# Attention weights applied to the tokens before Wv, Wv as the stationary operand, one pool of PSUM banks and a new order of stages

## The chip, the cores and the metric

The kernel runs on one core of one Trainium2 chip. The metric is the device time of one execution in microseconds. The engines are named as the profile names them: PE (TensorE, matmuls), PEld (its weight loads), DVE (VectorE), ACT (ScalarE), POOL (GpSimd) and SP (SyncE, which issues the weight DMAs).

## The reference

Four blocks run one after the other on x of shape 2048 x 640: memory attention A, local attention B, A again, B again. Each adds its result to x after a layer norm.

```python
# A: segments of 32 tokens, 8 memory tokens ahead of each; 32 heads of 192
for s in range(n_seg):                                # 64 segments
    h = concat([mem, xs], axis=1)                     # 40 x 640
    q, k, v = h @ Wq, h @ Wk, h @ Wv                  # per head 40 x 192
    scores = q @ k.T * scale                          # masked
    p = softmax(scores)                               # per head 40 x 40
    o = (p @ v) @ Wo                                  # sum over heads
    mem = o[:, :8, :]                                 # carried to the next segment
    outs.append(o[:, 8:, :])
# B: 32 heads of 20; each token attends to 8 positions, 2 apart
q, k, v = split(x @ wqkv)
o = softmax(sum(q * k[window])) * v[window] @ wo
```

The memory makes segment s + 1 of a block wait for segment s of the same block.

## The kernel before

One step handles one segment of both A blocks at once: segment s of the first and segment s - 2 of the second (`LAG`), as two "lanes" `l` of 40 rows, 80 columns in all. The state `ST` holds the tokens of both lanes transposed, 5 chunks of 128 features. There are 67 steps; the last one does B alone. The weights of A, 64 halves of 128 x 1920 bf16 (480 KB), don't fit: 31 stay in SBUF (`RESIDENT`), the other 33 are read again in each step through a ring of 5 buffers (`half`, L227 to L241, DMAs on SP's queue). In step 0 all come from the inputs, and the streamed ones are written to DRAM as they will be read (`Wr`).

The stages of a step, each named in `PLAN`:

- `q` (qk, 16 of them, two heads each): queries and keys; weights stationary, the 80 columns of `ST` moving; 30 matmuls; ACT copies the bank to a `QK` tile (L315).
- `s` (scores, 4, each for four q): 32 matmuls on parts of the array (L325, L331), then a softmax chain on DVE and ACT (L335 to L343) that ends in `Pm`.
- `t` (p_transpose, 4): four PE transposes, `Pm` to `PT`, copied out by DVE and then ACT (L352, L353).
- `v` (16): `ST` stationary, a half of Wv moving, 5 matmuls of 384 columns (L361); ACT or DVE copies out by turns (L365, L367).
- `pv` (4): v stationary in pieces of 64 columns, `PT` moving, 24 half-tile matmuls (L378) for two `ot` tiles, 96 in a step; ACT copies out (L381).
- `o` (16): a half of Wo stationary, `ot` moving, summed up in one PSUM tile `acc` over the whole step (L395).
- B, for the segments that the step before has finished: `ln1` (b_stats), `qkv`, `logits`, `e` (b_expand, 5), `wo`, `ln2` (beta_x), `store`; and `alpha` and `input` for new tokens.

PE runs in the order of `PLAN` as written (`manual_schedule(engines={PE})`). The other engines' orders are made at build time by the framework's scheduler from its own estimate of when each instruction is ready; at run time each engine goes through its queue in order. `COLUMNS` is a table of costs that only chooses which halves stay resident, so that the streamed ones are spread evenly over a step. PSUM has eight banks: pool psA has three (q, v and acc), psS three (s and pv), psB two (everything else). At the end of a step `finish_step` (L398) casts the memory rows of `acc` into the next `ST` (L405).

Of the kernel before, what the change touches and what calls it, by code (L numbers as in the profile page):

```python
# [10 lines left out]
BF16 = mybir.dt.bfloat16  # L11
F32 = mybir.dt.float32
# [3 lines left out]
PSUM = bass.MemoryType.PSUM  # L16
# [3 lines left out]
P = 128  # L20
D = 640
NCH = 5
# [3 lines left out]
NM = 8  # L26
SEG = 32
LT = NM + SEG
SLOT = 64
NP_ = 16  # L30
UW = 384
# [18 lines left out]

def stages():

    plan = [("q", 0), ("q", 1), ("alpha", 0), ("q", 2), ("q", 3), ("ln1", 0)]
    plan += [("q", 4), ("s", 0), ("v", 0), ("q", 5), ("v", 1), ("qkv", 0), ("q", 6), ("t", 0), ("v", 2), ("q", 7), ("v", 3)]
    for g in (2, 3):
        i, j = 4 * g, 2 * (g - 2)
        extra = [[], [], [("logits", 0)], [("input", 0)], []] if g == 2 else [[("e", c)] for c in range(5)]
        plan += [("q", i), ("s", g - 1), ("pv", g - 2)] + extra[0] + [("v", i - 4)] + extra[1] + [("q", i + 1)] + extra[2]
        plan += [("o", 2 * j), ("o", 2 * j + 1)] + extra[3] + [("v", i - 3), ("q", i + 2), ("t", g - 1), ("v", i - 2)] + extra[4]
        plan += [("o", 2 * j + 2), ("o", 2 * j + 3), ("q", i + 3), ("v", i - 1)]  # L60
    plan += [("s", 3), ("pv", 2), ("v", 12), ("v", 13), ("wo", 0), ("o", 8), ("o", 9), ("v", 14), ("v", 15), ("t", 3)]
    plan += [("o", 10), ("ln2", 0), ("pv", 3), ("o", 11), ("store", 0)]
    return plan + [("o", k) for k in range(12, 16)]
# [5 lines left out]
COLUMNS = {"q": 1200, "v": 1920, "o": 1200, "s": 2000, "pv": 1000, "t": 700, "ln1": 900, "ln2": 900, "qkv": 5000, "logits": 1000, "e": 500, "wo": 1700}  # L69


def resident_halves():

    order, t = [], 0
    for what, i in PLAN:
        for h in ([2 * i, 2 * i + 1] if what == "q" else [{"v": 32, "o": 48}[what] + i] if what in "vo" else [None]):
# [40 lines left out]
class Kernel:  # L117
    def __init__(self, ctx, tc, A_x, A_mem0, A_Wq, A_Wk, A_Wv, A_Wo, B_wqkv, B_wo, out):
        self.tc, self.nc = tc, tc.nc
        self.x = A_x[0, :, :]  # L120
        self.out = out[0, :, :]
        self.S = A_x.shape[1]
        self.n_seg = self.S // SEG
        self.Wq, self.Wk, self.Wv = (w.rearrange("d h e -> d (h e)") for w in (A_Wq, A_Wk, A_Wv))
        self.Wo = A_Wo.rearrange("h e d -> (h e) d")
        self.B_wqkv, self.B_wo, self.mem0 = B_wqkv, B_wo, A_mem0[0, :, :]
        pool = lambda name, bufs, **k: ctx.enter_context(tc.tile_pool(name=name, bufs=bufs, **k))
        self.cp = pool("consts", 1)
# [12 lines left out]
    def constants(self):  # L141
# [56 lines left out]
        self.PT = [cp.tile([P, 4, 2, 2, LT], BF16, name=f"PT{i}") for i in range(2)]  # L198
        for t in self.PT:
            nc.gpsimd.memset(t[:], 0.0)  # L200
# [5 lines left out]
        mt = self.psB.tile([P, NCH, NM], BF16, name="mt", tag="B")  # L206
# [46 lines left out]
    def input_tile(self, t):  # L253
# [12 lines left out]
        for k, src in enumerate((xn, x_sb)):  # L266
            tp = self.psB.tile([P, NCH, P], BF16, name="tp", tag="B")
# [12 lines left out]
    def ln_stats(self, src, n):  # L280
# [5 lines left out]
        ps = self.psB.tile([P, 2, n], F32, name="ln_ps", tag="B")  # L286
# [18 lines left out]
    def qk(self, i):  # L305
        nc = self.nc
        st = self.ST[self.step % 2]
        ps = self.psA.tile([P, 6, 2, LT], F32, name="qk_ps", tag="A")
# [8 lines left out]
    def scores(self, g):  # L317
        nc = self.nc
        ps = self.psS.tile([P, 4, 2, LT], F32, name="s_ps", tag="S")
# [14 lines left out]
        sb = self.w2.tile([P, 8, LT], F32, name="sb")  # L334
# [10 lines left out]

    def p_transpose(self, g):
        nc = self.nc
        ps = self.psB.tile([P, 4, 2, SLOT], BF16, name="pt_ps", tag="B")
        for j in range(4):
            nc.tensor.transpose(out=ps[:, j, :, :].rearrange("p h q -> p (h q)"),  # L350
                                in_=self.Pm[g % 2][:, j, :, :].rearrange("p l t -> p (l t)"), identity=self.ident[:, :])
        nc.vector.tensor_copy(out=self.PT[g % 2][0:64, :, :, 0, :], in_=ps[0:64, :, :, 0:LT])  # L352
        nc.scalar.copy(out=self.PT[g % 2][64:128, :, :, 1, :], in_=ps[64:128, :, :, 0:LT])  # L353

    def v(self, i):
        nc = self.nc
        w = self.half(32 + i)[:, :].rearrange("p (c n) -> p c n", c=NCH)
        st = self.ST[self.step % 2]
        ps = self.psA.tile([P, UW], F32, name="v_ps", tag="A")
        for c in range(NCH):  # L360
            nc.tensor.matmul(ps[:, :], lhsT=st[:, c, :, :].rearrange("p l t -> p (l t)"), rhs=w[:, c, :],  # L361
                             start=(c == 0), stop=(c == NCH - 1))
        vt = self.vp.tile([P, UW], BF16, name="vt")
        if i % 2 == 0:
            nc.scalar.copy(out=vt[:, :], in_=ps[:, :])  # L365
        else:
            nc.vector.tensor_copy(out=vt[:, :], in_=ps[:, :])  # L367
        self.vts[i] = vt

    def pv(self, g):  # L370
        nc = self.nc
        for k in (2 * g, 2 * g + 1):
            ps = self.psS.tile([P, 2, 3, 2, LT], F32, name="o_ps", tag="S")
            for jj in range(2):
                i = 2 * k + jj
                vt = self.vts.pop(i)
                for (n, slot, h, col) in ((0, 0, 0, 0), (0, 1, 0, 64), (1, 0, 0, 128), (1, 1, 1, 192), (2, 0, 1, 256), (2, 1, 1, 320)):
                    nc.tensor.matmul(ps[64 * slot:64 * (slot + 1), jj, n, :, :], lhsT=vt[:, col:col + 64], rhs=self.PT[g % 2][:, i % 4, h, :, :],  # L378
                                     start=True, stop=True, tile_position=(0, 64 * slot))
            ot = self.w3.tile([P, 6, 2, LT], BF16, name="ot")  # L380
            nc.scalar.copy(out=ot[:, :, :, :], in_=ps[:, :, :, :, :].rearrange("p j n l t -> p (j n) l t"))  # L381
            self.ots[k] = ot

    def o(self, jh):

        nc = self.nc
        j = jh // 2
        if jh == 0:
            self.acc = self.psA.tile([P, NCH, 2, LT], F32, name="acc", tag="A")
        ot = self.ots[j]  # L390
        for m in range(3 * (jh % 2), 3 * (jh % 2) + 3):
            if m % 3 == 0:
                w = self.half(48 + jh)[:, :].rearrange("p (m d) -> p m d", m=3)
# [30 lines left out]
    def b_qkv(self):  # L424
        nc = self.nc
        qT = self.w1.tile([P, NCH, 2, SEG], BF16, name="qT", tag="q")
        kh = self.w2.tile([P, NCH, 2, BPAD + SEG], BF16, name="kh")
        vh = self.w2.tile([P, NCH, 2, BPAD + SEG], BF16, name="vh")
        for new, old in ((kh, self.kh), (vh, self.vh)):
            if old is None:  # L430
                nc.gpsimd.memset(new[:, :, :, 0:BPAD], 0.0)
            else:
                nc.gpsimd.tensor_copy(out=new[:, :, :, 0:BPAD], in_=old[:, :, :, SEG:SEG + BPAD])
        for kind, dst in enumerate((qT[:, :, :, :], kh[:, :, :, BPAD:], vh[:, :, :, BPAD:])):
            ps = self.psB.tile([P, NCH, 2, SEG], F32, name="qkv_ps", tag="B")
# [5 lines left out]
        self.qT, self.kh, self.vh = qT, kh, vh  # L441
# [6 lines left out]
    def b_logits(self):  # L448
        nc = self.nc
        hf = SEG // 2  # L450
        ps = self.psB.tile([P, BW, hf], F32, name="lg_ps", tag="B")
# [25 lines left out]
    def b_expand(self, c):  # L477
        nc = self.nc
        ps = self.psB.tile([P, 2, BW, SEG], F32, name="bc_ps", tag="B")
# [7 lines left out]
    def b_wo(self):  # L487
        nc, s = self.nc, self.step
        ps = self.psB.tile([P, NCH, 2, SEG], F32, name="y_ps", tag="B")
# [22 lines left out]
    def store(self):  # L512
# [4 lines left out]
        ps = self.psB.tile([P, NCH, P], BF16, name="yt_ps", tag="B")  # L517
# [7 lines left out]
    def run(self):  # L525
        nc, tc = self.nc, self.tc
        self.resident, self.xt, self.vts, self.ots = {}, {}, {}, {}
        self.Wr = {h: self.dram.tile([P, HALF], BF16, name=f"Wr{h}") for h in range(N_HALVES) if h not in RESIDENT}
        self.kh = self.vh = None
        self.x2 = self.x2_next = None  # L530
        self.step = 0
        with tc.manual_schedule(engines={PE}):
# [5 lines left out]
            attend = {"q": self.qk, "s": self.scores, "t": self.p_transpose, "v": self.v, "pv": self.pv, "o": self.o}  # L538
            local = {"ln1": self.b_stats, "qkv": self.b_qkv, "logits": self.b_logits, "wo": self.b_wo, "ln2": self.beta_x, "store": self.store}
            for s in range(n_steps + 1):  # L540
# [10 lines left out]
                for what, i in PLAN:  # L551
                    if what in attend and a:
                        attend[what](i)
                    elif what in local and b:
# [64 lines left out]
```

## Time and profile before

| | |
|---|---|
| median of 3 runs | 3730.98 us (3726.68 to 3731.62) |
| span of the profiled execution | 3732.1 us; the page lists no time around it |
| PE busy | 3430.9 us (92%), 78045 matmuls |
| PEld busy | 2929.7 us (79%) |
| DVE busy | 2077.9 us (56%) |
| ACT busy | 1493.5 us (40%) |
| POOL busy | 365.5 us (10%) |
| granted PE clock | 0.984 on average, 1.00 from 200 to 3700 us |
| DMA | 1121.56 MB, 301 GB/s |
| casts of L405 that end the first and the last step with A | 144.89 and 3701.97 us |

Durations of one instruction are in its row of the page or of the groups by line and shape: 203 ns for a matmul of 80 columns, for example. Matmuls are pipelined, so a row's duration is not what one more of them costs; that is the distance from start to start, which the timeline gives. In the timeline, instructions of one kind that follow each other are merged into one row with their count, and the idle time before it stands in brackets with the engine that ended it.

### The profile page before, as it was taken

To read this page: it belongs to the slowest core of one execution; us is meant where nothing else is said; L and a number is where in the kernel's file an instruction comes from. 1 tells how busy PE (TensorE), PEld (TensorE's weight loads), DVE (VectorE), ACT (ScalarE), POOL (GpSimd) and SP (SyncE) were. 2 spreads that over 40 slices of the span, in tenths; PEclk is the share of its full clock that TensorE was granted. 3 is DMA by queue.
4 is the path that set the end of the run, shared out by engine and by line. 5 is a ranking of instruction groups with operands and counts; after the bars stand their busy time and mean duration, and the time that the engine had idled before them with its cause. 6 is when DMAs were issued, how large, how long until landed. Compare 5 with 4: busy or idle time off the path is not lost.

```text
span 3732.1 us, 170184 instructions
## 1 busy us (share of the span) xinstructions
PE 3430.9 (92%) x78045; PEld 2929.7 (79%) x78045; DVE 2077.9 (56%) x4858; ACT 1493.5 (40%) x3213; POOL 365.5 (10%) x467
## 2 busy tenths in 40 slices
PE   5799999999999999999999999999999999999997
PEld 3588788788788878778887887887888788788886
DVE  1355555655555555655556565555555555555555
ACT  1243444444444344444434444444443444444443
POOL 2110010011011001011100100100110010011000
PEclk7899999999999999999999999999999999999998
DMA  9988888888888889889888888888888888888885
GB/s 351 343 297 296 295 302 304 297 305 293 304 301 302 304 296 306 297 299 307 300 307 301 303 301 291 307 291 303 305 301 302 303 307 297 306 296 300 304 304 193
DMA packets 356064, 1121.56 MB, mean 301 GB/s; under 512 B 36424, under 2 KB 78032, under 8 KB 355344
## 3 DMA queue, kind: packets, MB, share of 16 engines
q1 hardware_dynamic: 350400, 1091.82, 86.2%
q0 software_dynamic: 2640, 16.22, 1.1%
q8 instruction: 610, 9.99, 1.1%
q10 hardware_dynamic: 2304, 2.62, 0.2%
q14 instruction: 110, 0.90, 0.1%
HBM read 1091.68 MB, written 18.84 MB: 298 GB/s over the span
## 4 chain that ended last, share of the span: by engine, by line
PE 66%; DVE 21%; DMA 7%; ACT 2%; issue 2%; SPq 1%; POOLq 0%; DVEq 0%; POOL 0%; ACTq 0%
PE qk_ps L313 23%; PE v_ps L361 18%; PE acc L395 11%; DVE oT L485 5%; DVE prod L483 4%; PE qkv_ps L438 4%; PE s_ps L331 3%; PE s_ps L325 2%; DVE vt L367 2%; PE o_ps L378 2%; DMA x_sb<-in_A_x_dram 2%; DMA wt<-Wr 2%; PE y_ps L492 1%; DVE sb L335 1%; DVE mx L337 1%
## 5 line engine op out<-in xcount | busy, mean ns | idle before, releaser
L315 ACT CAST QK<-qk_ps 128x480 bf16<-128x480 f32 x1056 | 586.9, 556 | 1197.9 <-PE qk_ps L313 1190.2
L313 PE MATMUL qk_ps<-ST,res 128*128 128x80 bf16 x17820 | 800.2, 203 | 56.1 <-DVE ST L405 21.3
L361 PE MATMUL v_ps<-wt,ST 128*128 128x384 bf16 x3630 | 706.2, 328 | 134.8 <-DVE vt L367 124.3
L313 PEld LDWEIGHTS <-res 128*128 128x128 bf16 x17820 | 724.8, 100 | 97.9 <-issue 49.4
L361 PEld LDWEIGHTS <-ST 128*128 128x128 bf16 x5280 | 475.0, 99 | 410.5 <-issue 150.3
L313 PE MATMUL qk_ps<-ST,wt 128*128 128x80 bf16 x13860 | 646.8, 203 | 15.8 <-DMA wt<-in_A_Wq_dram 8.0
L313 PEld LDWEIGHTS <-wt 128*128 128x128 bf16 x13860 | 575.9, 100 | 68.7 <-DMA wt<-in_A_Wq_dram 9.0
L367 DVE CAST vt<-v_ps 128x384 bf16<-128x384 f32 x528 | 289.8, 549 | 542.8 <-PE v_ps L361 541.4
L395 PE MATMUL acc<-ot,wt 128*128 128x80 bf16 x7920 | 375.8, 203 | 17.8 <-DMA wt<-in_A_Wo_dram 6.7
L395 PE MATMUL acc<-ot,res 128*128 128x80 bf16 x7920 | 364.3, 203 | 11.2 <-issue 6.0
L395 PEld LDWEIGHTS <-res 128*128 128x128 bf16 x7920 | 328.4, 100 | 42.0 <-DMA res<-in_A_Wo_dram 7.1
L365 ACT CAST vt<-v_ps 128x384 bf16<-128x384 f32 x528 | 250.1, 474 | 266.4 <-PE v_ps L361 262.2
L395 PEld LDWEIGHTS <-wt 128*128 128x128 bf16 x7920 | 317.7, 100 | 30.8 <-issue 8.6
L381 ACT CAST ot<-o_ps 128x480 bf16<-128x480 f32 x528 | 275.0, 560 | 162.2 <-PE o_ps L378 162.1
L485 DVE TENSOR_REDUCE oT<-prod 128x64 bf16<-128x512 bf16 x330 | 335.1, 1016 | 2.2
L361 PE MATMUL v_ps<-res,ST 128*128 128x384 bf16 x1650 | 328.4, 330 | 6.2 <-DMA res<-in_A_Wv_dram 4.2
L445 POOL TENSOR_TENSOR prod<-qT,kh 128x1280 bf16<-128x1280 bf16 x66 | 204.4, 3097 | 684.1 <-ACT kh L440 684.1
L335 DVE TENSOR_TENSOR sb<-s_ps,maskA 128x320 f32<-128x320 f32 x264 | 129.3, 490 | 212.3 <-PE s_ps L331 212.3
L283 POOL TENSOR_TENSOR sq<-x 128x160 f32<-128x160 bf16 x64 | 28.9, 452 | 2095.3 <-DVE x L496 2095.3
L483 DVE TENSOR_TENSOR prod<-bc_ps,vh 128x512 bf16<-128x512 f32 x330 | 222.8, 675 | 9.9 <-PE bc_ps L480 1.6
L353 ACT COPY PT<-pt_ps 64x320 bf16<-64x320 bf16 x264 | 110.9, 420 | 242.0 <-DVE PT L352 239.1
L341 DVE TENSOR_REDUCE sm<-sb 128x8 f32<-128x320 f32 x264 | 127.7, 484 | 107.2 <-ACT sb L339 107.2
(113 smaller groups left out, 3320.1 us busy)
## 6 DMA issues: line engine op xcount, KB each, us to landing
wt<-Wr SPq DMA_DIRECT2D x2145, 480.0 KB, 5.2
Wr<-wt POOLq DMA_DIRECT2D x33, 480.0 KB, 6.7
wt<-in_A_Wv_dram SPq DMA_DIRECT2D x11, 480.0 KB, 10.3
res<-in_A_Wk_dram SPq DMA_DIRECT2D x9, 480.0 KB, 10.7
res<-in_A_Wq_dram SPq DMA_DIRECT2D x9, 480.0 KB, 10.4
wt<-in_A_Wo_dram SPq DMA_DIRECT2D x8, 480.0 KB, 9.1
res<-in_A_Wo_dram SPq DMA_DIRECT2D x8, 480.0 KB, 10.0
wt<-in_A_Wq_dram SPq DMA_DIRECT2D x7, 480.0 KB, 11.0
```

The costliest lines, as they stand in the source:

```text
L313: nc.tensor.matmul(ps[:, 3 * k + m, :, :], lhsT=w[:, c, m * P:(m + 1) * P], rhs=st[:, c, :, 0:LT], start=(c == 0), stop=(c == NCH - 1))
L315: nc.scalar.copy(out=self.QK[i % NQK][:, 0:12 * LT], in_=ps[:, :, :, :].rearrange("p m l t -> p (m l t)"))
L335: nc.vector.tensor_tensor(out=sb[:, :, :], in0=sv, in1=self.maskA[:, :].unsqueeze(1).to_broadcast([P, 8, LT]), op=ALU.add)
L361: nc.tensor.matmul(ps[:, :], lhsT=st[:, c, :, :].rearrange("p l t -> p (l t)"), rhs=w[:, c, :], start=(c == 0), stop=(c == NCH - 1))
L365: nc.scalar.copy(out=vt[:, :], in_=ps[:, :])
L367: nc.vector.tensor_copy(out=vt[:, :], in_=ps[:, :])
L381: nc.scalar.copy(out=ot[:, :, :, :], in_=ps[:, :, :, :, :].rearrange("p j n l t -> p (j n) l t"))
L395: nc.tensor.matmul(self.acc[:, dc, :, :], lhsT=w[:, m % 3, dc * P:(dc + 1) * P], rhs=ot[:, m, :, :], start=(j == 0 and m == 0 and dc == 0) ...
L438: nc.tensor.matmul(ps[:, d, :, :], lhsT=self.wqkv[:, c, kind * D + d * P:kind * D + (d + 1) * P], rhs=self.xnB[:, c, :].rearrange("p (l t) ...
L445: eng.tensor_tensor(out=self.prod[:, :, l, :, :], in0=qT[:, :, l, :].unsqueeze(2).to_broadcast([P, NCH, BW, SEG]), in1=window(kh, l), op=A ...
L483: nc.vector.tensor_tensor(out=pv, in0=ps[:, :, :, :], in1=window1(self.vh, c), op=ALU.mult)
L485: nc.vector.tensor_reduce(out=self.oT[:, c, :].rearrange("p (l t) -> p l t", l=2), in_=pv.rearrange("p l w t -> p l t w"), op=ALU.add, axi ...
```

## The change

The values of a head are no longer made for all tokens and then weighted. Since (P h) Wv equals P (h Wv), the step now forms U = P h for each head and multiplies it by Wv.

- A stage `h` transposes `ST` back once a step (5 transposes, one ACT copy), to `hT` with tokens on partitions.
- A stage `u` (8, four heads each) takes `hT` as the stationary operand, 64 rows (one lane) by 128 features, and `PT` of that lane as the moving one, 160 columns; the two lanes use the upper and the lower rows of the array and different PSUM banks. ACT copies lane 0 out, DVE lane 1, in two pieces each.
- A stage `v` (8, two halves of Wv each) holds Wv stationary and moves U, 80 columns. A half has 192 columns for each of two heads: 128 of each go as a full tile, the remaining 64 of both heads share the array as two column halves. The result is `ot` itself, so `pv` is gone.
- `PT` is copied by ACT alone, without the zero blocks that it had.
- `acc` has a PSUM bank of its own, and the other seven form one pool.
- `o` has 8 stages of 30 matmuls where it had 16 of 15.
- `kh` and `vh` have one buffer each in place of two, and POOL moves the edge within it.
- `PLAN` is a written list, in another order: among others s0 to s3 now stand right behind q3 with ln1, q7, q11 and q15.

```diff
+ORDER = """
+q0 h0 q1 alpha0 q2 q3 ln10 s0 q4 q5 qkv0 q6 t0 q7 s1
+u0 q8 v0 logits0 u1 q9 input0 v1 t1 o0 q10 e0 u2 q11 s2 e1 v2 o1 u3 e2 q12 v3 q13 e3 o2 t2 q14 e4 u4 q15 s3
+v4 u5 o3 v5 wo0 o4 t3 o5 u6 ln20 u7 v6 store0 v7 o6 o7
+"""
...
-COLUMNS = {"q": 1200, "v": 1920, "o": 1200, "s": 2000, "pv": 1000, "t": 700, "ln1": 900, "ln2": 900, "qkv": 5000, "logits": 1000, "e": 500, "wo": 1700}
+COLUMNS = {"q": 1200, "v": 1300, "o": 1200, "s": 2000, "u": 800, "t": 700, "ln1": 900, "ln2": 900, "qkv": 5000, "logits": 1000, "e": 500, "wo": 1700}
...
-        self.vp = pool("vp", 6)
-        self.psA = pool("psA", 3, space=PSUM)
-        self.psS = pool("psS", 3, space=PSUM)
-        self.psB = pool("psB", 2, space=PSUM)
+        self.up = pool("up", 2)
+        self.psC = pool("psC", 1, space=PSUM)
+        self.ps = pool("ps", 7, space=PSUM)
...
+    def h_transpose(self):
+        nc = self.nc
+        st = self.ST[self.step % 2]
+        ps = self.ps.tile([P, NCH, P], BF16, name="ht_ps", tag="ps")
+        for c in range(NCH):
+            nc.tensor.transpose(out=ps[:, c, :], in_=st[:, c, :, :].rearrange("p l t -> p (l t)"), identity=self.ident[:, :])
+        nc.scalar.copy(out=self.hT[:, :], in_=ps[:, :, :].rearrange("p c d -> p (c d)"))
...
-        nc.vector.tensor_copy(out=self.PT[g % 2][0:64, :, :, 0, :], in_=ps[0:64, :, :, 0:LT])
-        nc.scalar.copy(out=self.PT[g % 2][64:128, :, :, 1, :], in_=ps[64:128, :, :, 0:LT])
...
+        nc.scalar.copy(out=self.PT[g % 2][:, :, :, :], in_=ps[:, :, :, 0:LT])
+
+    def u(self, k):
+        nc = self.nc
+        pt = self.PT[(k // 2) % 2][:, 2 * (k % 2):2 * (k % 2) + 2, :, :].rearrange("p j h q -> p (j h q)")
+        u = self.up.tile([P, NCH, 4, 2, LT], BF16, name="u")
+        for c0, c1 in ((0, 3), (3, 5)):
+            ps = [self.ps.tile([P, c1 - c0, 4, LT], F32, name=f"u_ps{l}", tag="ps") for l in range(2)]
+            for c in range(c0, c1):
+                for l in range(2):
+                    r = slice(SLOT * l, SLOT * (l + 1))
+                    nc.tensor.matmul(ps[l][:, c - c0, :, :].rearrange("p h q -> p (h q)"), lhsT=self.hT[r, c * P:(c + 1) * P], rhs=pt[r, :],
+                                     start=True, stop=True, tile_position=(SLOT * l, 0))
+            nc.scalar.copy(out=u[:, c0:c1, :, 0, :], in_=ps[0][:, :, :, :])
+            nc.vector.tensor_copy(out=u[:, c0:c1, :, 1, :], in_=ps[1][:, :, :, :])
+        self.us[k] = u
+
+    def v(self, k):
+        nc = self.nc
+        u = self.us.pop(k)
+        ps = self.ps.tile([P, 2, 3, 2, LT], F32, name="o_ps", tag="ps")
+        for jj in range(2):
+            w = self.half(32 + 2 * k + jj)[:, :].rearrange("p (c n) -> p c n", c=NCH)
+
+            def whole(n, h):
+                for c in range(NCH):
+                    nc.tensor.matmul(ps[:, jj, n, :, :], lhsT=w[:, c, P * n:P * (n + 1)], rhs=u[:, c, 2 * jj + h, :, :],
+                                     start=(c == 0), stop=(c == NCH - 1), skip_group_check=True)
+
+            def split():
+                for c in range(NCH):
+                    for h in range(2):
+                        nc.tensor.matmul(ps[SLOT * h:SLOT * (h + 1), jj, 1, :, :], lhsT=w[:, c, P + SLOT * h:P + SLOT * (h + 1)], rhs=u[:, c, 2 * jj + h, :, :],
+                                         start=(c == 0), stop=(c == NCH - 1), tile_position=(0, SLOT * h), skip_group_check=True)
+
+            if jj == 0:
+                whole(0, 0)
+                whole(2, 1)
+                split()
+            else:
+                split()
+                whole(0, 0)
+                whole(2, 1)
+        ot = self.w3.tile([P, 6, 2, LT], BF16, name="ot")
+        nc.scalar.copy(out=ot[:, :, :, :], in_=ps[:, :, :, :, :].rearrange("p j n l t -> p (j n) l t"))
...
-            self.acc = self.psA.tile([P, NCH, 2, LT], F32, name="acc", tag="A")
+            self.acc = self.psC.tile([P, NCH, 2, LT], F32, name="acc")
...
-        kh = self.w2.tile([P, NCH, 2, BPAD + SEG], BF16, name="kh")
-        vh = self.w2.tile([P, NCH, 2, BPAD + SEG], BF16, name="vh")
...
+        kh, vh = self.kh, self.vh
+        if self.step > 1:
+            for t in (kh, vh):
+                nc.gpsimd.tensor_copy(out=t[:, :, :, 0:BPAD], in_=t[:, :, :, SEG:SEG + BPAD])
```

The softmax's `sb` tile also goes from two buffers to one.

More of the change, by code (lines that the diff above doesn't have):

```diff
@@ L48 @@
 RING = 5
-def stages():
[L53 to L63, printed above, removed]
+ORDER = """
[3 more added lines that the diff above has]
+"""
+def stages():
+    names = ("alpha", "ln1", "qkv", "logits", "input", "wo", "ln2", "store", "q", "h", "s", "t", "u", "v", "o", "e")
+    plan = []
+    for word in ORDER.split():
+        what = next(n for n in names if word.startswith(n) and word[len(n):].isdigit())
+        plan.append((what, int(word[len(what):])))
+    return plan
 PLAN = stages()
-COLUMNS = {"q": 1200, "v": 1920, "o": 1200, "s": 2000, "pv": 1000, "t": 700, "ln1": 900, "ln2": 900, "qkv": 5000, "logits": 1000, "e": 500, "wo": 1700}
+COLUMNS = {"q": 1200, "v": 1300, "o": 1200, "s": 2000, "u": 800, "t": 700, "ln1": 900, "ln2": 900, "qkv": 5000, "logits": 1000, "e": 500, "wo": 1700}
 def resident_halves():
@@ L75, in resident_halves @@
     for what, i in PLAN:
-        for h in ([2 * i, 2 * i + 1] if what == "q" else [{"v": 32, "o": 48}[what] + i] if what in "vo" else [None]):
+        first = {"q": 0, "v": 32, "o": 48}.get(what)
+        for h in ([None] if first is None else [first + 2 * i, first + 2 * i + 1]):
             t += COLUMNS.get(what, 0)
@@ L197, in constants @@
             nc.gpsimd.memset(t[:], 0.0)
-        self.PT = [cp.tile([P, 4, 2, 2, LT], BF16, name=f"PT{i}") for i in range(2)]
-        for t in self.PT:
+        self.PT = [cp.tile([P, 4, 2, LT], BF16, name=f"PT{i}") for i in range(2)]
+        self.hT = cp.tile([P, D], BF16, name="hT")
+        self.kh = cp.tile([P, NCH, 2, BPAD + SEG], BF16, name="kh")
+        self.vh = cp.tile([P, NCH, 2, BPAD + SEG], BF16, name="vh")
+        for t in (self.kh, self.vh):
             nc.gpsimd.memset(t[:], 0.0)
@@ L307, in qk @@
         st = self.ST[self.step % 2]
-        ps = self.psA.tile([P, 6, 2, LT], F32, name="qk_ps", tag="A")
+        ps = self.ps.tile([P, 6, 2, LT], F32, name="qk_ps", tag="ps")
         for k in range(2):
@@ L318, in scores @@
         nc = self.nc
-        ps = self.psS.tile([P, 4, 2, LT], F32, name="s_ps", tag="S")
+        ps = self.ps.tile([P, 4, 2, LT], F32, name="s_ps", tag="ps")
         for j in range(4):
@@ L351, in p_transpose @@
                                 in_=self.Pm[g % 2][:, j, :, :].rearrange("p l t -> p (l t)"), identity=self.ident[:, :])
-        nc.vector.tensor_copy(out=self.PT[g % 2][0:64, :, :, 0, :], in_=ps[0:64, :, :, 0:LT])
-        nc.scalar.copy(out=self.PT[g % 2][64:128, :, :, 1, :], in_=ps[64:128, :, :, 0:LT])
-    def v(self, i):
+        nc.scalar.copy(out=self.PT[g % 2][:, :, :, :], in_=ps[:, :, :, 0:LT])
+    def u(self, k):
         nc = self.nc
[L357 to L368, printed above, removed]
@@ L370, in pv @@
-    def pv(self, g):
-        nc = self.nc
[L372 to L382, printed above, removed]
@@ L386, in o @@
+    def o(self, j):
         nc = self.nc
-        j = jh // 2
-        if jh == 0:
-            self.acc = self.psA.tile([P, NCH, 2, LT], F32, name="acc", tag="A")
+        if j == 0:
+            self.acc = self.psC.tile([P, NCH, 2, LT], F32, name="acc")
         ot = self.ots[j]
-        for m in range(3 * (jh % 2), 3 * (jh % 2) + 3):
+        for m in range(6):
             if m % 3 == 0:
-                w = self.half(48 + jh)[:, :].rearrange("p (m d) -> p m d", m=3)
+                w = self.half(48 + 2 * j + m // 3)[:, :].rearrange("p (m d) -> p m d", m=3)
@@ L426, in b_qkv @@
         qT = self.w1.tile([P, NCH, 2, SEG], BF16, name="qT", tag="q")
[L427 to L433 removed]
+        kh, vh = self.kh, self.vh
+        if self.step > 1:
+            for t in (kh, vh):
+                nc.gpsimd.tensor_copy(out=t[:, :, :, 0:BPAD], in_=t[:, :, :, SEG:SEG + BPAD])
         for kind, dst in enumerate((qT[:, :, :, :], kh[:, :, :, BPAD:], vh[:, :, :, BPAD:])):
[L435 removed]
+            ps = self.ps.tile([P, NCH, 2, SEG], F32, name="qkv_ps", tag="ps")
             for d in range(NCH):
@@ L478, in b_expand @@
         nc = self.nc
-        ps = self.psB.tile([P, 2, BW, SEG], F32, name="bc_ps", tag="B")
+        ps = self.ps.tile([P, 2, BW, SEG], F32, name="bc_ps", tag="ps")
         nc.tensor.matmul(ps[:, :, :, :].rearrange("p l w t -> p (l w t)"), lhsT=self.ET[:, c, :],
@@ L553, in run @@
                         attend[what](i)
+                    elif what == "h" and a:
+                        self.h_transpose()
                     elif what in local and b:
```

24 lines of the change are left out of this document (11 added, 13 removed).

## The prediction

> **What bounds the kernel now.** I read the page first, then the waits of TensorE (PE), then the timeline of one steady step for PE, VectorE (DVE) and ScalarE (ACT). A step is the time from one DVE cast of L405 (`ST<-acc`) to the next; the timeline has the first at 144.89 and the last at 3701.97, so 65 steps of 54.72 us lie between a load-bound first step (145 us) and a tail of 30 us. The change acts on these 65.
>
> Page, busy time and chain:
>
> ```profile
> PE 3430.9 (92%) x78045; PEld 2929.7 (79%) x78045; DVE 2077.9 (56%) x4858; ACT 1493.5 (40%) x3213; POOL 365.5 (10%) x467
> ...
> PE 66%; DVE 21%; DMA 7%; ACT 2%; issue 2%; SPq 1%; POOLq 0%; DVEq 0%; POOL 0%; ACTq 0%
> ```
>
> PE sets the time, but a fifth of the chain is DVE. The waits of PE (total us, times, longest) say where DVE enters:
>
> ```profile
> PE v_ps L361 <- DVE vt L367: 124.3, 115, 1.5
> ...
> PE o_ps L378 <- ACT PT L353: 13.9, 65, 0.6
> ```
>
> The timeline (start, us, engine, line, tiles, count) gives the prices, as start of one group to start of the next:
>
> ```profile
> 1847.90 0.70 PE L313 MATMUL qk_ps<-ST,wt 128*128 128x80 bf16 x15
> ...
> 1863.48 0.70 PE L313 MATMUL qk_ps<-ST,res 128*128 128x80 bf16 x15
> 1864.11 0.43 PE L325 MATMUL s_ps<-QK 64*64 64x40 bf16 x16
> 1864.47 0.43 PE L331 MATMUL s_ps<-QK 128*64 128x40 bf16 x16
> 1864.74 0.60 PE L378 MATMUL o_ps<-PT,vt 128*64 128x80 bf16 x24
> 1865.28 0.99 PE L361 MATMUL v_ps<-wt,ST 128*128 128x384 bf16 x5
> 1866.10 0.70 PE L313 MATMUL qk_ps<-ST,wt 128*128 128x80 bf16 x15
> 1866.63 0.70 PE L313 MATMUL qk_ps<-ST,res 128*128 128x80 bf16 x15
> ...
> 1881.74 0.98 PE L361 MATMUL v_ps<-res,ST 128*128 128x384 bf16 x5
> ...
> 1883.62 0.39 PE L350 MATMUL pt_ps<-ident,Pm 128*128 128x128 bf16 x4
> 1885.54 0.97 PE L361 MATMUL v_ps<-wt,ST 128*128 128x384 bf16 x5 [1.53 <-DVE vt L367]
> ```
>
> - 15 full-tile matmuls of 80 columns take 0.535 us, 36 ns each; 5 of 384 take 0.82, 163 ns each. The line through both is 0.418 ns a column plus 2.5.
> - 24 of 80 columns on half tiles (128*64) take 0.54 with the way out; a full-to-half change is paid at both ends: 1863.48 + 15 x 0.036 = 1864.02, and s starts at 1864.11, about 0.10 late. Without that 0.10 the 24 take 0.44: two halves of the array run at once, 36 ns a pair.
> - So each change of tile shape costs about 0.10; s (L325, L331: 0.36 less 0.10, and 0.27, for 8 pairs) goes at 32 to 34 ns a pair.
>
> The last two lines are the wait: transposes of 0.22 us, then v stands until DVE empties a v_ps. DVE and ACT at those times:
>
> ```profile
> 1883.43 1.00 DVE L485 TENSOR_REDUCE oT<-prod 128x64 bf16<-128x512 bf16 x1
> 1884.36 0.67 DVE L483 TENSOR_TENSOR prod<-bc_ps,vh 128x512 bf16<-128x512 f32 x1
> 1884.95 0.54 DVE L367 CAST vt<-v_ps 128x384 bf16<-128x384 f32 x1
> ...
> 1848.64 0.56 ACT L315 CAST QK<-qk_ps 128x480 bf16<-128x480 f32 x1 [3.22 <-PE qk_ps L313]
> ```
>
> The v matmuls of 1881.74 end at 1882.72, but DVE, in order behind `b_expand`, empties them from 1884.95: 2.23 late. The eight DVE evacuations of v in this step start 1.18, 0.04, 1.10, 0.04, 2.23, 0.04, 0.58 and 0.04 late, mean 0.65; the late ones met a softmax, logits, `b_expand` or LN chain.
>
> **The change, part by part, per step.**
>
> *Removed on PE.* v: 80 matmuls x 163 = 13.04 us. pv: 96 half-tile matmuls, 48 pairs x 36 = 1.73. Together 14.77.
>
> *Added on PE.* New v: per half of Wv 10 full matmuls and 5 pairs, 16 halves: 160 x 36 + 80 x 36 = 8.64. u: 80 matmuls on 64-row tiles, 160 columns; by the line above one takes 69 ns. The trace has no 64*128 tile. If the pair on rows 0-63 and 64-127 runs at once, as column halves do and as the 64*64 pairs of L325 do (both rows and columns differ there), 40 x 69 = 2.76; if one after the other, 5.52. I take 2.76. h: 5 transposes x 56 (pt_ps, 4 in 0.22) = 0.28. Together 11.68, so 3.09 less.
>
> [...]
>
> *Tile-shape changes.* Before: each s goes in, over (64*64 to 128*64) and out, 12 in all, pv0 to pv2 riding in the shape that s leaves; pv3 adds two and logits two: 16. After: s again 12, logits 2, the half tiles of eight v 16, eight u 16; less two, because u0 follows s1 and u1 follows logits0 directly and out and in are one change: 44. The record's 132 ns from start to start at such a place, against 36 inside a group, makes one 0.096. So 28 x 0.096 = 2.69 more.
>
> [...] If the 64*128 shape were excepted, some 15 changes fell out and the forecast were about 94 us lower.
>
> *Waits removed.* The t-to-v wait goes: v_ps no longer exists, and q, u, v, s and B share seven banks instead of two free ones (acc held the third of psA). 124.3 us in 115 waits plus the 0.17 that the record's modelled end hides in each is 144, 2.18 a step. pv3's wait for PT (13.9 + 65 x 0.17, 0.37 a step) goes too: o5 (30 matmuls, 1.08) lies between t3 and u6, over ACT's single copy, about 0.42 by the row of L353. Together 2.55.
>
> *Wait added, q to s.* In the new order q3, q7, q11 and q15 stand directly (q3 but for ln1) before s0 to s3, which read that q as their fourth tile. A q's last matmul starts at 1847.90 + 14 x 0.036 = 1848.40, its ACT copy at 1848.64 and ends 1849.20: 0.80, with the hand-over 0.85. s has the change of shape and one start (0.13) and 6 pairs x 0.032 = 0.32 to do before it needs tile four. So 0.53 for s1, s2 and s3, about 0.1 for s0: 1.7 a step. Before, another q or v stood between. All of PE is queued behind it; ACT is otherwise free there.
>
> *Wait added, u to v.* v(k) needs all of u(k), which ACT and DVE now bring out in two copies each. DVE: 480 and 320 columns, from the rows for 384 (549 ns) and 80 (241): 0.65 and 0.48. First group ready 0.41 after u starts, so done at best at 1.6. v asks for its fourth chunk at 0.45 + 1.08 (one q or o between) + 0.11 = 1.64. There is no slack: each late DVE start is a PE stall. v2 and v4 have an s between and are covered; v0, v1, v3, v5, v6, v7 are not, and each meets a chain: s1's, logits', s2's with `b_expand`, s3's, ln2's twice. Bounds: 6 x 0.04 = 0.24, and 6 x 1.3 (mean of the four late starts) = 7.7. Laid out by hand, with DVE alternating between chain and u copy as it does between softmax and `b_expand` around 1878 to 1884, I get 0.7, 0.5, 0.8, 0.3, 0.4, 0.3: 3.0, nearer to six times the mean start of 0.65 (3.9) than to either end. I take 3.0.
>
> *At nothing.* DVE gains 8 x 1.13 and loses 8 x 0.55 and 4 x 0.31 (PT): 31.5 + 3.4 of some 56; ACT gains 8 x 0.98 + 0.69 (hT) and loses 8 x 0.47: neither is a bound by its sum. The kh and vh edge copies on POOL (0.30 each) wait for the last reader in the same buffer, done well before the next qkv0; if not, ACT's kh waits 0.6. The same 33 halves a step stream through SP's queue; `wt<-Wr` cost PE 4.2 us in all, and a longer step asks less of DMA (301 GB/s now). hT (0.69 by the row of L521, the same size) has some twelve microseconds before u0.
>
> *Sum.* -3.09 + 2.69 - 2.55 + 1.7 + 3.0 = +1.75 us a step; 65 steps: +114. The profiled run's span is 3732.1, 1.1 above the median of 3730.98, with no other time around it on the page. 3731 + 114 = **3845**.
>
> **Rivals.**
> - *Copies prompt, faster.* If DVE takes each u copy when it is ready, the last wait is 0.24 and the step 1.0 shorter: 3665. It decides at a u-to-v total of 1.25 a step. For it: four of eight starts were 0.04 late, and the new order shifts the chains. Against: every uncovered v has a chain beside it.
> - *Row tiles in series.* 2.76 more a step: 3845 + 179 = 4025. Against: every pair of disjoint tiles in the trace overlaps.
> - *DVE chain always first.* 7.7 in place of 3.0: +305, about 4150. For it: at 1857 vt stood behind three softmax pieces. Against: the alternation above.
> - *The seven banks don't free v's path*: another evacuation takes the t-to-v wait's place in the rotation, 2.18 a step back: 3990.
>
> **How the numbers follow.** Forecast, late copies (1.25 to about 5.2 a step; slower): 0.62. Prompt copies: 0.27. Series 0.05, chain first 0.03, banks 0.03. The range 3690 to 3990 runs from copies at 0.6 a step to copies at 5.2; it leaves out about 0.1 of the prompt case and most of the last three. A measurement tells about 0.2% (7.5 us, 0.115 a step): copies between 1.13 and 1.36, 0.04, half from the first case and half from the second. So faster 0.25, slower 0.60 + 0.11 = 0.71.
>
> **What would show it.** In the profile after: PE waits `o_ps <- DVE u` of 80 to 340 us as the largest, `s_ps <- ACT QK` around 100; u's 10 matmuls in 0.35 us plus 0.10 at each side, v in about 1.28; no v_ps-type wait after pt_ps; step about 56.5. Wrong if `o_ps` hardly waits for DVE (then faster), or if u's 10 take 0.7.

## The result: 7% slower, and the profile after

The changed kernel takes 3993.35 us (median of four, 3990.89 to 3994.53) against 3731.3 before: a ratio of 1.070, interval 1.0685 to 1.0715. Its profiled execution spans 3991.3 us. That is slower, as forecast, but by 262 us and not by 114, and 3 us above the range. The first step (145 us) and the tail (30 us) stayed; the 65 steps between went from 54.72 to 58.70 us each (casts of L432 at 145.2 and 3960.9).

The page of the changed kernel, PE's busy time, the instruction queue and the chain:

```profile
PE 3573.1 (90%) x93159; PEld 3212.8 (80%) x93159; DVE 2225.3 (56%) x5122; ACT 1773.1 (44%) x3807; POOL 373.8 (9%) x465
...
q8 instruction: 728, 11.93, 1.2%
...
PE 63%; DVE 19%; DMA 7%; ACT 5%; issue 4%; SPq 1%; POOLq 0%; ACTq 0%; DVEq 0%; POOL 0%
```

PE still has the largest share of the chain, but 15114 matmuls more, and "issue", time in which the profile shows nothing waited for, has grown from 2% to 4%. PE's waits after:

```profile
PE s_ps L330 <- ACT QK L320: 80.6, 205, 1.5
PE qk_ps L318 <- DVE ST L432: 67.8, 64, 5.0
PE o_ps L391 <- DVE u L379: 63.9, 201, 0.6
PE qk_ps L318 <- issue: 37.6, 38, 2.8
PE o_ps L391 <- ACT u L378: 20.0, 62, 0.3
PE acc L422 <- issue: 11.4, 15, 1.7
PE qkv_ps L462 <- issue: 11.3, 13, 1.6
```

The first, third and fifth are the two waits that the prediction added. The wait for DVE's u is 63.9 us here, less than the 80 to 340 that the prediction named, and not the largest; the view counts idle time behind the modelled end of a matmul, which is shorter than the distance from start to start in the table below. The second was 21.3 us before. The lines that end in "issue" sum to 87 us over the whole view, 33 before. The wait for vt is gone.

The timeline of PE in one step:

```profile
1709.42 0.52 PE L376 MATMUL u_ps<-PT,hT 64*128 64x160 bf16 x10
1709.87 0.39 PE L503 MATMUL bc_ps<-attn,ET 128*128 128x512 bf16 x1
1710.10 0.70 PE L318 MATMUL qk_ps<-ST,wt 128*128 128x80 bf16 x15
1710.63 0.70 PE L318 MATMUL qk_ps<-ST,res 128*128 128x80 bf16 x15
1711.64 0.27 PE L391 MATMUL o_ps<-u,wt 128*128 128x80 bf16 x3 [0.30 <-DVE u L379]
1712.35 0.42 PE L391 MATMUL o_ps<-u,wt 128*128 128x80 bf16 x7 [0.44 <-DVE u L379]
1712.71 0.37 PE L397 MATMUL o_ps<-u,wt 128*64 128x80 bf16 x10
1712.91 0.35 PE L397 MATMUL o_ps<-u,res 128*64 128x80 bf16 x10
1713.19 0.53 PE L391 MATMUL o_ps<-u,res 128*128 128x80 bf16 x10
...
1719.16 0.36 PE L330 MATMUL s_ps<-QK 64*64 64x40 bf16 x12
1719.88 0.24 PE L330 MATMUL s_ps<-QK 64*64 64x40 bf16 x4 [0.35 <-ACT QK L320]
...
1727.46 0.27 PE L422 MATMUL acc<-ot,wt 128*128 128x80 bf16 x3
1729.34 0.59 PE L422 MATMUL acc<-ot,wt 128*128 128x80 bf16 x12 [1.60 <-issue]
```

- u's ten matmuls take 0.45 with the way out: five pairs at 70 ns, so the two row tiles run at once.
- v stops at its first and again at its fourth chunk, where DVE's two copies of u end; its twenty half-tile matmuls take 0.48 with the change of shape.
- s stops after 12 of 16, at the fourth q.
- In the last two lines `acc` stops after three matmuls of fifteen with the same weights and the same `ot`: no data can be late there. 1.6 us pass without a releaser.

At the end of one step in four, PE, DVE and ACT after:

```profile
726.49 0.70 PE L422 MATMUL acc<-ot,res 128*128 128x80 bf16 x15
730.80 0.70 PE L318 MATMUL qk_ps<-ST,res 128*128 128x80 bf16 x15 [3.61 <-DVE ST L432]
...
724.84 0.34 ACTq L545 DMA_DIRECT2D out_dram<-yo  x1
...
730.16 0.45 DVE L269 TENSOR_SCALAR xn<-x_sb,lnst 128x640 bf16<-128x640 bf16 x1 [6.03 <-DMA out_dram<-yo]
730.52 0.23 DVE L432 CAST ST<-acc 128x80 bf16<-128x80 f32 x1
```

DVE's queue has the next input tile's `xn` ahead of the cast that starts the next step. `xn` shares one buffer with `yo`, which ACT has just sent out; DVE stands for 6 us until that DMA has landed, and PE behind it.

Such a stop can be followed by a stretch of slow matmuls. At the end of another step:

```profile
494.07 0.70 PE L422 MATMUL acc<-ot,res 128*128 128x80 bf16 x15
498.69 1.16 PE L318 MATMUL qk_ps<-ST,res 128*128 128x80 bf16 x15 [3.92 <-DVE ST L432]
499.65 1.20 PE L318 MATMUL qk_ps<-ST,wt 128*128 128x80 bf16 x15
500.65 0.73 PE L356 MATMUL ht_ps<-ident,ST 128*128 128x128 bf16 x5
...
503.91 0.70 PE L318 MATMUL qk_ps<-ST,res 128*128 128x80 bf16 x15
504.45 0.70 PE L318 MATMUL qk_ps<-ST,wt 128*128 128x80 bf16 x15
```

From 499.65 to 500.65 the fifteen matmuls of 80 columns go at 67 ns from start to start, from 503.91 at 36 again: the clock granted to PE is 0.50 from 496.8 to 503.6 us, and 1.00 behind it. Between 200 us and the last cast the changed kernel has 23 such stretches of 3.4 or 6.8 us, 105.8 us in all; the kernel before has 3, 10.2 us. Those of the 60 steps in the table below, 22, follow a stop of PE of 1.0 to 5.2 us that began at most 5.5 us earlier: ten times the wait for the cast, seven times a wait without a releaser, five times the wait of s for QK. Not every such stop is followed by one.

From the trace I took each distance from start to start, less the price of the first matmul (36 ns for 80 columns and so on), and put it down to the place where it lies; us a step, 60 steps, before to after:

| | forecast | measured |
|---|---|---|
| PE work | -3.09 | 48.75 to 45.70: -3.05 |
| changes of shape (16 to 44) | +2.69 | 1.51 to 4.18: +2.67 |
| waits of v for vt, pv3 for PT | -2.55 | 2.45 to 0: -2.45 |
| s waits for QK | +1.7 | +1.9 |
| v waits for u | +3.0 | +2.8 |
| block borders of 256 instructions | none | 0.68 to 1.70: +1.0 |
| end of step, ST | none | 0.50 to 1.27: +0.8 |
| the rest, most of it between q matmuls at half the granted clock | none | +0.4 |
| step | +1.75 | 54.70 to 58.77: +4.07 |

Counted by itself, the extra time of matmuls at half the granted clock (distances between two of one kind, less that kind's price at full clock) is 0.05 us a step before and 0.60 after. That is enough for the whole of the rest; the rows of this account are good to about 0.1 to 0.2 us.

### The profile page after: what moved, and what is told of

It reads as the page before. It is cut to its first block, busy times and chain, and to the rows that moved or that the text cites. A ratio compares the mean times of both kernels' runs of the same rounds, so it can differ in the third digit from the quotient of the medians.

```text
span 3991.3 us, 201812 instructions
## 1 busy us (share of the span) xinstructions
PE 3573.1 (90%) x93159; PEld 3212.8 (80%) x93159; DVE 2225.3 (56%) x5122; ACT 1773.1 (44%) x3807; POOL 373.8 (9%) x465
## 3 DMA queue, kind: packets, MB, share of 16 engines
q8 instruction: 728, 11.93, 1.2%
q10 hardware_dynamic: 2304, 2.62, 0.2%
## 4 chain that ended last, share of the span: by engine, by line
PE 63%; DVE 19%; DMA 7%; ACT 5%; issue 4%; SPq 1%; POOLq 0%; ACTq 0%; DVEq 0%; POOL 0%
PE qk_ps L318 24%; PE acc L422 10%; PE o_ps L391 8%; DVE u L379 5%; PE o_ps L397 4%; PE u_ps L376 3%; PE qkv_ps L462 3%; ACT QK L320 3%; PE s_ps L336 2%; DVE sb L340 2%; PE s_ps L330 2%; DVE mx L342 2%; DVE sm L346 2%; DMA out_dram<-yo 2%; ACT sb L344 2%
## 5 line engine op out<-in xcount | busy, mean ns | idle before, releaser
L318 PE MATMUL qk_ps<-ST,wt 128*128 128x80 bf16 x16830 | 782.9, 204 | 39.0 <-issue 27.8
L318 PE MATMUL qk_ps<-ST,res 128*128 128x80 bf16 x14850 | 698.2, 205 | 99.7 <-DVE ST L432 67.8
L318 PEld LDWEIGHTS <-wt 128*128 128x128 bf16 x16830 | 679.9, 101 | 74.4 <-issue 33.3
L379 DVE CAST u<-u_ps 128x480 bf16<-128x480 f32 (+1 forms) x1056 | 584.7, 559 | 156.6 <-PE u_ps L376 155.8
L378 ACT CAST u<-u_ps 128x480 bf16<-128x480 f32 (+1 forms) x1056 | 472.5, 494 | 181.9 <-PE u_ps L376 168.7
L391 PE MATMUL o_ps<-u,wt 128*128 128x80 bf16 x5940 | 359.8, 204 | 102.5 <-DVE u L379 63.6
L391 PEld LDWEIGHTS <-wt 128*128 128x128 bf16 x5940 | 265.3, 100 | 174.5 <-DVE u L379 82.6
L422 PEld LDWEIGHTS <-wt 128*128 128x128 bf16 x6930 | 285.3, 101 | 20.3 <-issue 7.5
L376 PE MATMUL u_ps<-PT,hT 64*128 64x160 bf16 x5280 | 280.5, 233 | 3.1 <-issue 1.9
L391 PE MATMUL o_ps<-u,res 128*128 128x80 bf16 x4620 | 259.4, 205 | 5.1 <-issue 2.9
L330 PE MATMUL s_ps<-QK 64*64 64x40 bf16 x4224 | 158.0, 188 | 86.8 <-ACT QK L320 80.6
L344 ACT ACTIVATE sb<-sb 128x320 f32<-128x320 f32 x264 | 124.2, 470 | 224.3 <-DVE sb L343 218.9
```

The lines of the kernel that those rows point to most:

```text
L318: nc.tensor.matmul(ps[:, 3 * k + m, :, :], lhsT=w[:, c, m * P:(m + 1) * P], rhs=st[:, c, :, 0:LT], start=(c == 0), stop=(c == NCH - 1))
L330: nc.tensor.matmul(ps[hs, j, l, :], lhsT=rows(q[hs, :], 4, l), rhs=keys(q[hs, :], 1, l), start=(j == 0 and l == 0), stop=False, tile_posit ...
L376: nc.tensor.matmul(ps[l][:, c - c0, :, :].rearrange("p h q -> p (h q)"), lhsT=self.hT[r, c * P:(c + 1) * P], rhs=pt[r, :], start=True, sto ...
L378: nc.scalar.copy(out=u[:, c0:c1, :, 0, :], in_=ps[0][:, :, :, :])
L379: nc.vector.tensor_copy(out=u[:, c0:c1, :, 1, :], in_=ps[1][:, :, :, :])
L391: nc.tensor.matmul(ps[:, jj, n, :, :], lhsT=w[:, c, P * n:P * (n + 1)], rhs=u[:, c, 2 * jj + h, :, :], start=(c == 0), stop=(c == NCH - 1) ...
```

## The experiments

Theory A: the forecast's terms hold, and the excess is the two rows that it had not. Rival B: DVE's queue as a whole is behind, and what is taken away at one place is stood at another.

**A buffer of its own for yo.**

```diff
-        yo = self.w1.tile([P, D], BF16, name="yo", tag="xn")
+        yo = self.w1.tile([P, D], BF16, name="yo")
```

> The changed kernel with a buffer of its own for yo, the tile that store writes out; nothing else differs. Theory A (the sum of the prediction holds and waits outside it make up the rest): DVE's xn of the next input tile, queued ahead of the cast of ST, no longer waits for the output DMA, so the long waits of q0 for the cast (67.8 us in all, up to 5.0) fall back to about 21 us as in the kernel before; 0.77 us a step less, 65 steps, about 50 us: 3943. Rival B (DVE's queue as a whole is behind, and what is taken away at one place is stood elsewhere): 3980 or more.

3952.22 us, 41 less. PE's wait for the cast:

```profile
PE qk_ps L318 <- DVE ST L432: 21.2, 64, 0.3
```

It is back where it was before the change, and the end of a step at 0.50. The ten stretches at half clock that followed this wait are gone too: ten stretches are left of 22, and their price fell from 0.60 to 0.21 us a step. The shared buffer is shown as a cause. The two gains make 1.2 us a step, of which 0.7 are left in the step: the waits for u and for instructions took about 0.2 each.

**s one stage later.**

```diff
-q3 ln10 s0 q4 ... q7 s1 u0 q8 ... q11 s2 e1 v2 o1 ... q15 s3 v4 u5
+q3 ln10 q4 s0 ... q7 u0 s1 q8 ... q11 e1 v2 s2 o1 ... q15 v4 s3 u5
```

> The changed kernel with each s one stage later, behind q4, u0, v2 and v4, so that no s follows directly on its own q. Theory A: the waits of s_ps for ACT's QK copy (1.9 us a step from start to start) go, 124 us; v2 and v4 lose the cover that s gave them and v0 wins some, net up to 60 us back: 3870 to 3930. Rival B (the wait only hid the lateness of DVE's u copies): the wait of o_ps for u grows by as much, 3980 or more.

4006.0 us, no gain. PE's waits:

```profile
PE o_ps L391 <- DVE u L379: 141.6, 242, 1.0
...
PE pt_ps L363 <- DVE Pm L348: 61.5, 39, 1.9
```

The wait for QK fell from 1.9 to 0.2 us a step, but v's wait for u rose from 2.8 to 3.6, and t now waits 1.05 for `Pm`: no gain in all. Rival B is right here: the two added waits are not independent. s, softmax, t and u are one chain, and where s comes later, its DVE part runs later too: the waits that grew are those for DVE's `Pm` and u.

**v without half tiles.** (The last 64 columns of a half's second head are left out.)

```diff
             def split():
                 for c in range(NCH):
-                    for h in range(2):
-                        nc.tensor.matmul(ps[SLOT * h:SLOT * (h + 1), jj, 1, :, :], lhsT=w[:, c, P + SLOT * h:P + SLOT * (h + 1)], ...
+                    nc.tensor.matmul(ps[:, jj, 1, :, :], lhsT=w[:, c, P:2 * P], rhs=u[:, c, 2 * jj, :, :], ...
```

> The changed kernel with the two half-tile matmuls of a pair in v replaced by one full-tile matmul of the same 80 columns. It leaves out the last 64 columns of the second head of each half, so its output is not the reference's. PE's time in the pairs stays 36 ns each; the 16 changes of tile shape of v go, and 80 of 1411 matmuls. Theory A: 16 x 0.096 = 1.54 us a step less, 100 us, and perhaps 10 to 20 us of instruction supply: about 3880. Rival (the changes of shape run while PE would wait for u anyway): 3960 or more.

3873.98 us, 119 less. Changes of shape fell from 44 to 28 and from 4.18 to 2.61 us a step (102 us), waits at block borders from 1.70 to 1.50 (13 us). So each of these changes of shape did cost its 0.10; PE did not run them in time that it would have waited anyway.

**The pool alone, on the kernel before.**

```diff
-        self.psA = pool("psA", 3, space=PSUM)
-        self.psS = pool("psS", 3, space=PSUM)
-        self.psB = pool("psB", 2, space=PSUM)
+        self.psC = pool("psC", 1, space=PSUM)
+        self.ps = pool("ps", 7, space=PSUM)
```

> The kernel before with one part of the change alone: acc in a bank of its own and one pool of seven PSUM banks for everything else. Theory A: the wait of v behind the transposes (2.19 us a step from start to start) goes: 142 us less, about 3590. Rival (another late evacuation takes its place in the rotation of seven): within 30 us of 3731.

3582.69 us, ratio 0.9604 (0.9582 to 0.9626). The wait for vt is gone from its view of waits. One part of the change is worth 148 us by itself, and this kernel beats both; set against it, the other parts of the change together cost 411 us.

**Half of the streamed weights.**

```diff
+        if self.step > 0:
+            self.turn += 1
+            if self.turn % 2 == 0:
+                return self.last
-        t = self.ring.tile([P, HALF], BF16, name="wt")
+        t = self.last = self.ring.tile([P, HALF], BF16, name="wt")
```

> The changed kernel with half of the streamed weights: from step 1 on every second streamed half is not read, and the tile of the one before is used in its place, so its output is not the reference's. PE's instructions and their order stay. In the trace of the changed kernel every wait of PE without a releaser, above 0.32 us, stands at an instruction whose number is 193 modulo 256, 1.2 to 1.6 us behind the end of a 16 KB transfer of the instruction queue: 98 us in 96 waits, against 43 in 46 before. Theory A (instruction blocks arrive late because their transfers queue with the weights): with half the weight traffic most of the 98 us and the few waits for wt go, 3880 to 3910. Rival (a fixed cost at every block of 256 instructions): the waits stay, 3985 or more.

3823.87 us, 169 less. PE's instructions are the same. The longest waits now:

```profile
PE o_ps L395 <- DVE u L383: 91.7, 310, 0.6
PE s_ps L334 <- ACT QK L324: 69.9, 199, 0.4
PE qk_ps L322 <- DVE ST L436: 40.4, 64, 2.9
```

Waits that end in "issue" sum to 0.2 us, from 87. A block border is no fixed cost here: PE waits at it with all of the weight traffic (282 GB/s) and hardly with half of it (156 GB/s). The gain exceeds what the account has at the borders (1.70 x 65 = 110 us): DVE's `xn` waits less for the output DMA too (54.9 us, from 82.7; PE's wait for the cast is the third line, and the end of a step fell from 1.27 to 0.82), and with fewer long stops the time at half clock fell from 105.8 to 10.2 us, its price from 0.60 to 0.07 us a step.

**v reads a constant tile.**

```diff
-        self.us[k] = u
+        self.us[k] = self.ufix
```

> The changed kernel with v reading a constant tile instead of u; u's matmuls and copies are still made (into one buffer), but nobody waits for them, so the output is not the reference's. Theory A: the waits of v for u's copies (2.77 us a step from start to start) go and little comes back: 180 us, about 3815. Rival (DVE's lateness only moves, to t, to the PSUM rotation or to the end of the step, as it did when the s stages were moved): less than 60 us, 3935 or more.

3912.02 us, 81 less, not 180. v's wait went from 2.8 to 0.2 us a step, but the block borders rose from 1.70 to 2.62. Neither theory had this: most of what comes back is not stood on DVE but in the supply of instructions.

**Another order.** yo as above, and:

```diff
-q0 h0 q1 alpha0 q2 q3 ln10 s0 q4 q5 qkv0 q6 t0 q7 s1
-u0 q8 v0 logits0 u1 q9 input0 v1 t1 o0 q10 e0 u2 q11 s2 e1 v2 o1 u3 e2 q12 v3 q13 e3 o2 t2 q14 e4 u4 q15 s3
-v4 u5 o3 v5 wo0 o4 t3 o5 u6 ln20 u7 v6 store0 v7 o6 o7
+q0 h0 q1 alpha0 q2 q3 ln10 s0 q4 q5 qkv0 q6 t0 q7 u0 s1
+q8 u1 v0 logits0 q9 input0 v1 t1 o0 q10 e0 q11 u2 s2 u3 e1 v2 o1 e2 q12 v3 q13 e3 o2 t2 q14 e4 q15 u4 s3
+u5 o3 v4 v5 wo0 t3 o4 u6 ln20 u7 o5 v6 store0 v7 o6 o7
```

> The changed kernel with yo's own buffer and another order: u0, u2 and u4 stand between q and s (they cover the wait of s for QK and come ahead of the softmax on DVE), every v has at least one stage more behind its u, and o5 stands between u7 and v6. Theory A, from the account of the changed kernel's trace: 41 us for yo as measured, 1.8 us a step of q to s and about 2.2 of u to v: 260 us, in all 3690, between 3640 and 3760. Rival (softmax and copies bind on DVE whatever the order, as the moved s stages suggest): 3850 or more.

3861.59 us. PE's longest waits:

```profile
PE qk_ps L318 <- issue: 73.9, 82, 3.0
PE o_ps L397 <- issue: 30.3, 37, 2.3
PE acc L422 <- issue: 28.3, 44, 2.5
PE o_ps L391 <- issue: 21.3, 26, 1.9
PE qk_ps L318 <- DVE ST L432: 21.2, 64, 0.3
```

The waits for QK (0.6 a step) and u (0.2) are nearly gone, as theory A had it, but "issue" sums to 223 us, and 116 us at half clock cost 0.68 us a step. Rival B is wrong here: DVE can keep up. The supply has taken the place of both.

**The same order with half of the streamed weights.** (The edit of the half-weights run on the kernel above.)

> The reordered kernel (e6_order) with every second streamed half left unread and the tile of the one before used in its place; its output is not the reference's. In e6_order the waits for QK, for u and for yo are nearly gone (s 0.6, v 0.2 us a step), and 4.1 us a step stand at the block borders of 256 instructions instead. Theory A (supply of instructions, 11.0 blocks a step, is what binds there): those 4.1 us go, 270 us, about 3595. Rival (another resource stands behind it, DVE above all): 3700 or more.

3515.3 us, below even the expected 3595; "issue" sums to 0.5 us and no other wait came in. More than half of the 80 us beyond theory A is the clock: this run has no stretch at half clock between 200 us and the last cast, 0.68 us a step less. It reads half the weights, so it isn't to be set against the kernels that read all; it says that PE and DVE could do this order in 51.3 us a step.

**More instructions in the kernel before.** On the kernel with the pool:

```diff
-            nc.tensor.matmul(ps[:, :], lhsT=st[...], rhs=w[:, c, :], ...
+            for a in range(3):
+                nc.tensor.matmul(ps[:, P * a:P * (a + 1)], lhsT=st[...], rhs=w[:, c, P * a:P * (a + 1)], ...
```

> The kernel before with the pool of seven banks (e4_before_pool), and each v matmul of 384 columns as three of 128, each with its own weight load: 160 more matmuls a step, 5 ns x 80 = 0.4 us more work, the same columns and the same DMAs. 2365 PE instructions a step become 2685, 9.2 blocks of 256 become 10.5, 5.0 us each without waits where it was 5.6. Theory A (waits at block borders by us per block, as 5.18 gave 1.7, 4.98 gave 2.6 and 4.79 gave 4.1 us a step): some 2.3 us a step where there was about 0.85, with the work 1.9 us, +120: about 3700. Rival (the waits belong to the new kernel's kinds of instruction, not to their number): +26, about 3610.

> e9_v_in_three with every second streamed half unread, its output not the reference's. Theory A: no waits at block borders, 52.0 us a step, about 3550, below e4_before_pool in spite of 160 more matmuls. Rival (more matmuls cost time of their own beyond 5 ns x 80): 3610 or more.

3740.84 us with all weights, 158 more than with whole v matmuls, and 3532.88 with half of them. PE's longest waits with all weights:

```profile
PE qk_ps L312 <- issue: 42.2, 56, 2.3
PE acc L395 <- issue: 28.7, 36, 2.7
PE v_ps L361 <- issue: 27.1, 32, 2.1
```

"issue" sums to 134 us, from 40. No new kind of instruction, no new wait on data, only 320 PE instructions a step more: their number does it, with all of the weight traffic. The price is above what theory A expected (120). With half the weights it runs in 51.6 us a step, below the 52.4 of the kernel with whole v matmuls and all weights.

**pv3 later, on the kernel with the pool.**

```diff
-    plan += [("o", 10), ("ln2", 0), ("pv", 3), ("o", 11), ("store", 0)]
+    plan += [("o", 10), ("ln2", 0), ("o", 11), ("pv", 3), ("store", 0)]
```

> e4_before_pool with pv3 one stage later, behind o11 instead of ln2, so that ACT's copy of PT lies beside o11. Theory A: the 0.25 us a step that pv3 waits for PT go, 16 us: about 3567. Rival (the wait is taken up by o12, which needs pv3's copy): 3580 to 3590.

3602.92 us, 20 more. The wait for PT (14.1 us in 64 waits) is gone, and the next o now waits for pv's copy, `acc` for ACT's ot (39.3 us in 66 waits): the rival's mechanism, with a higher price than it gave.

**A shallower ring, on the other order.**

```diff
-N_RESIDENT = 31
-RING = 5
+N_RESIDENT = 32
+RING = 4
```

> e6_order with a ring of 4 buffers in place of 5 and the freed space used for one more resident half (32 resident, 32 streamed): fewer bytes of weights are in flight at any time, and 3% fewer are read. Theory A (a block of instructions waits behind the weights that are in flight): the waits without a releaser fall from 223 us to about 120, in all about 3760. Rival (the delay does not depend on the depth of the queue, or PE waits for weights instead): 3850 or more.

3865.31 us, no change. "issue" fell from 223 to 91 us. Part of that could be due to blocks that take longer, but at the same time for a block there are fewer gaps too: behind blocks run through in 4.0 to 4.8 us, 94 gaps in 351 cases, where e6_order had 188 in 445. So the depth of the weights' ring does bear on how late a block comes; but PE now waits for the weights:

```profile
PE acc L422 <- DMA wt<-Wr: 59.7, 65, 2.8
PE qk_ps L318 <- DMA wt<-Wr: 34.5, 65, 2.2
...
PE o_ps L397 <- DMA wt<-Wr: 24.7, 30, 1.7
```

Both theories had half of it.

## Why the prediction was wrong in size and right in direction

- *PE work and changes of shape* came out to 0.04 us a step. The row tiles overlap: 70 ns a pair, and not the 138 of one after the other. The 64*128 shape pays for its changes as the others do (medians from start to start in the trace of after: 134 ns from a full tile into it, against 36 inside a full-tile group; 162 out of it, against 70 a pair), and the 16 changes that `e3_no_half_tiles` left out were worth 0.098 us each.
- *Waits removed* were right, and `e4_before_pool` shows the larger one causally (148 us; forecast 142 of the 166).
- *Waits added* were right in sum (1.9 for 1.7, 2.8 for 3.0) and in place: v2 and v4 hardly wait, as foreseen. That the sum for u is so close is in part luck. Stage by stage it missed both ways: v0 waits 0.3 us where it had 0.7, v6 0.1 where it had 0.4, and v5 0.7 where it had 0.3. The prediction also added these waits as if each could be taken away by itself; the runs show that moving s alone only moves its wait to u and t.
- *The step that failed is "At nothing".* It counted DMA by bytes ("a longer step asks less of DMA") and the added PE instructions by their time from start to start alone; it gave no price to their supply, to a shared buffer or to the stretches at half clock that follow long stops. Instructions a step went from 9.2 to 11.0 blocks of 256, and the borders cost 1.0 us a step more. The same paragraph dealt with buffers for `kh` and `vh`, but did not look at `store0` and `input0`, which moved as well: the groups of before, by line and shape, already had DVE's `xn` wait 34.6 us for the output DMA, at a place where it cost PE nothing; in the new order it waits 82.7 us, ahead of the cast (0.8 us a step, 41 us by `e1_own_yo`). The remaining 0.4 is for the most part matmuls at half the granted clock: they take 0.60 us a step more than at full clock, 0.05 before; with yo's own buffer 0.21, with half the weights 0.07.
- *The rival "copies prompt, faster"* would have come out wrong even where it held: `e6_order` has prompt copies, and is 3861.59 where the rival had 3665, because the supply binds next.

The slowdown is thus a sum, a step: 2.8 us won (less work and fewer old waits, less the changes of shape), 4.7 of new waits on data, 0.8 for a shared buffer, 1.0 for the supply and 0.4 of the rest, mostly half clock, 4.1 in all. Behind the data waits the supply stands as a second bound: in `e6_order`, where waits for QK and u are down to 0.8 us a step, 4.1 us a step stand at the block borders, from 1.70.

## What to carry to other kernels

Price a change in matmuls and weight loads as well as in columns: where this core streamed all its weights (280 to 290 GB/s), no kernel with 11 blocks of 256 PE instructions a step came under 56.7 us a step, whatever else was mended. Before rewriting the arithmetic, take the waits off the profile one at a time: the pool of banks alone gave 4%. Look through the tags: two tiles that share a buffer tie a DMA of one stage to the queue of an engine in another (DVE stood 6.03 us for it above, and `e1_own_yo` was 41 us faster). And where a stretch of matmuls has gone slow with no wait in it (67 ns each for 36 here), read the granted clock there and the stop ahead of it.

## What the runs showed of the hardware

The page of the changed kernel has 728 transfers and 11.93 MB in instruction queue q8, 16 KB each; its trace has 186590 PE instructions (93159 matmuls, as many weight loads, 272 others), 256 to a transfer. The kernel before has 610 transfers for 156162, again 256. Such 256 are called a block here. In the changed kernel 95 of the 96 waits of PE above 0.32 us that had no semaphore between 250 and 3650 us (in the kernel before all 46) stand at the same place of a block, instruction 193 modulo 256 of the trace, and end 1.2 to 1.6 us after such a transfer does (one 3.4). Whether they occur goes with the time for the block before: behind blocks run through in 4.0 to 4.4 us there was a gap above 0.32 us at the border in 24 of 59 cases, in 4.8 to 5.2 us in 44 of 277, above 5.6 us in none of 94. The transfer itself takes 0.98 us (median), but starts 1.9 us into the block with all weights and 0.7 us with half of them (medians).

The last column is the time at a granted clock of 0.5 between 200 us and the last cast. In before and after, matmuls of 80 columns go at 67 ns from start to start there, at 36 ns elsewhere (medians).

| kernel | blocks a step | "issue", us | half clock, us |
|---|---|---|---|
| before | 9.2 | 33 | 10 |
| e4_before_pool | 9.2 | 40 | 3 |
| e9_v_in_three | 10.5 | 134 | 21 |
| after | 11.0 | 87 | 106 |
| e1_own_yo | 11.0 | 97 | 34 |
| e7_fixed_u | 11.0 | 135 | 123 |
| e6_order | 11.0 | 223 | 116 |
| e5, e8, e10 (half the weights) | 11.0, 11.0, 10.5 | 0.2, 0.5, 1.1 | 10, 0, 0 |
